# A decode block on one core: two bias vectors moved from the first load to sixteen short loads behind w1, and six other loads merged

## The chip, the cores and the metric

The program runs on one core of one Trainium2 chip. The metric is the device time of one execution in microseconds (us). It was run twice: 1054.84 and 1056.1 us, median 1055.47 us. A further execution was profiled; its own time was 1055.74 us and its span, from the first to the last instruction, 1053.9 us.

## The reference

One token passes through a transformer block with adaptive layer norms. Six modulation vectors come from a condition `c`. Attention has 32 heads of width 192 over a cache of 8192 positions; behind it comes a dense layer with a squared relu. All is float32.

```python
mod = (silu(c) @ w_mod).reshape(1, 6, 1, 640)
sa, ca, ga, sb, cb, gb = (mod[:, i] for i in range(6))
h = layernorm(x) * (1 + ca) + sa
q = (h @ wq) per head                    # 32 heads x 192
p = softmax(q . k_cache * 192 ** -0.5)   # over 8192 positions
x = x + ga * ((p @ v_cache) @ wo)
h = layernorm(x) * (1 + cb) + sb
f = max(h @ w1 + b1, 0) ** 2             # 640 -> 1536
x = x + gb * (f @ w2 + b2)               # 1536 -> 640
```

The key and value caches are by far the most of the data: 64 arrays of 6144 KB.

## The kernel before

**Staging.** Everything that is streamed goes through three large buffers (`slot`, line 53), 128 partitions of 14208 floats each. They are used in turn: the first load, then k0, v0, k1, v1 and so on to k31, v31, then `wm1_t`, `w1_t` and `w2_t`. A buffer can be loaded again only when the work on its old content is done. So wm1 follows v30 in its buffer, w1 follows k31, and w2 follows v31. All loads are issued from SyncE (SP) in program order and go into one DMA queue. A load of 128 partitions gives each partition one contiguous row.

**Counters of the loads.** The framework gives every load one of eight counters, DMAHW0 to DMAHW7, in turn: load number n (from 0) has counter n modulo 8. Who needs the data waits for that counter. Before SP issues a load on a counter, SP also waits until the load that had that counter last has landed, unless SP has already waited for it for another reason. A wait on SP holds back every load behind it in program order.

**A head (lines 201 to 275).** `keys` multiplies the head's keys by the query on VectorE (DVE, line 212) and sums the products on DVE, GpSimd (POOL) and ScalarE (ACT), in pieces that `SUMS` gives; the last head works in four pieces of 16 positions. `softmax` follows, `values` multiplies by the value cache on TensorE (PE, lines 248 and 252), and `own` brings the parts of the sums together. The key buffer of an odd head also holds a piece of `wo` behind the keys, which `gather` (line 154) uses; the last head's `gather` is what frees k31's buffer.

**How loads are cut.** `K_PARTS` cuts the key loads of the last two heads, line 98 the last value load in two, line 315 wm1 in two, `W1_CUT` w1 in two, and `W2_CUT` w2 in four pieces of 6, 3, 2 and 1 blocks. The sixth of the modulation matrix that makes `gb` (called wg here) has a load of its own behind w1, in w1's buffer (line 324).

**Biases.** `b1` and `b2` lie as 17 columns at the end of the first load. `bbc` (line 164) takes them out of its buffer, and `spread` (line 108: a copy and a transpose on DVE) makes them rows, `bbt`, at the start of the program (line 197).

**The end.** After the last head PE computes `ps_mod` from wm1 (line 335), the last attention sums and their projection `att` (341, 344), then, after a layer norm, `ps_f` from w1 (361). DVE adds `bbt`, squares and transposes to `fT` (364 to 366). PE computes `ps_g` from wg (371) and `ps_y` from w2 and `fT` (383); DVE makes `y`, and SP stores it (388). PE works in program order, so `ps_y` cannot start ahead of `ps_g`. Each matmul of float32 is two passes in the profile.

Of the kernel before, what the change touches and what calls it, by code (L numbers as in the profile page):

```python
# [14 lines left out]
D = 640  # L15
H = 32
SK = 8192
DH = 192
FF = 1536
# [3 lines left out]
KB = DG // 32  # L23
FB = FG // 32
PW = 2 * DH
NPAIR = H // 2
NPOS = SK // P
KV = NPOS * DH
WO = 3 * D
WQ = KB * PW  # L30
ROW = KV + WO
WM = KB * 2 * D
VEC = 3 * KB + FB
DA = 128
DB = DH - DA
REP = 8
K_PARTS = {H - 2: 2, H - 1: 4}
SUMS = {H - 3: ((14, 10), (14, 6)), H - 2: ((14, 12), (14, 8)), H - 1: ((4, 7), (4, 7), (4, 7), (4, 5))}
W1_CUT = ((0, 3), (3, 2))
W2_CUT = ((0, 6), (6, 3), (9, 2), (11, 1))  # L40
EPS = 1e-5


@with_exitstack
def block_kernel(ctx: ExitStack, tc: tile.TileContext, first, kx, vx, wm1, w1, w2, out):
    nc = tc.nc
    const = ctx.enter_context(tc.tile_pool(name="const", bufs=1))
    strm = ctx.enter_context(tc.tile_pool(name="strm", bufs=3))
# [4 lines left out]
    def slot(name):  # L53
        return strm.tile([P, ROW], F32, tag="slot", name=name, bufs=3)

    def big(name, n):
# [3 lines left out]
    k_t, v_t = {}, {}  # L60
    first_t = slot("first_t")
    nc.sync.dma_start(first_t[:, :WM + WQ + VEC], first)

# [11 lines left out]
                            axis=AX.X, op=ALU.add)  # L75
# [3 lines left out]
                            axis=AX.X, op=ALU.add)  # L79
# [3 lines left out]

    vec = first_t[:, WM + WQ:WM + WQ + VEC]
    c_c = vec[:, :KB]
    x_c = const.tile([P, KB], F32, name="x_c")
    bbc = const.tile([P, FB + KB], F32, name="bbc")

    def load_k(h):
        k_t[h] = slot(f"k{h}")  # L90
        n = K_PARTS.get(h, 1)
        cuts = [KV * c // n for c in range(n)] + [ROW if h not in (1, H - 2) else KV]
# [2 lines left out]

    def load_v(h):
        v_t[h] = slot(f"v{h}")
        cuts = (0, NPOS * DA, KV) if h == H - 1 else (0, KV)
        for a, b in zip(cuts, cuts[1:]):
            nc.sync.dma_start(v_t[h][:, a:b], vx[h, :, a:b])  # L100

    def columns(src, n, name, pool=const, **how):

# [4 lines left out]
    def spread(src, n, name):  # L108

        t = work.tile([P, FB + KB, 32], F32, name=name + "_c", tag="spread", bufs=1)  # L110
        nc.vector.tensor_copy(t[:, :n], src[:, :, None].to_broadcast([P, n, 32]))
        r = const.tile([P, 32 * n], F32, name=name)
        nc.vector.transpose(r, t[:, :n].rearrange("p b r -> p (b r)"))
        return r
# [46 lines left out]
    nc.vector.reciprocal(e, e)  # L161
    nc.vector.tensor_mul(e, e, c_c)
    nc.vector.tensor_copy(x_c, vec[:, KB:2 * KB])
    nc.vector.tensor_copy(bbc, vec[:, 2 * KB:])

    ma_w = big("ma_w", 2 * D)
    weigh(ma_w, first_t[:, :WM].rearrange("p (b n) -> p b n", b=KB))
# [26 lines left out]

    query(0, first_t[:, WM:WM + WQ])
    x_t = spread(x_c, KB, "x_t")
    bbt = spread(bbc, FB + KB, "bbt")

    ri_t, o_t, sp_t, os_t, sum_t = {}, {}, {}, {}, {}

# [22 lines left out]
    def softmax(h, sc):  # L223
        mp = work.tile([P, 1], F32, tag="mp", name=f"mp{h}")
        nc.vector.tensor_reduce(mp, sc, axis=AX.X, op=ALU.max)  # L225
        ps = psum.tile([P, 512], F32, tag="sm", name=f"ps_mx{h}", bufs=2)
        nc.tensor.transpose(ps[:, :P], mp.to_broadcast([P, P]), ident)  # L227
        nm = work.tile([P, 1], F32, tag="nm", name=f"nm{h}")
        nc.vector.tensor_reduce(nm, ps[:, :P], axis=AX.X, op=ALU.max, negate=True)  # L229

        p = work.tile([P, NPOS, REP], F32, tag="p", name=f"p{h}", bufs=1)
        i = h // 2
        if h % 2 == 0:
            sp_t[i] = work.tile([P, 2], F32, tag="sp", name=f"sp{i}")
        nc.scalar.activation(p, sc[:, :, None].to_broadcast([P, NPOS, REP]), AF.Exp, bias=nm,  # L235
                             accum_out=sp_t[i][:, h % 2:h % 2 + 1])
        if h % 2:
            sum_t[i] = total(sp_t.pop(i), f"sum{i}")
        return p
# [48 lines left out]
    for h in range(H):  # L288
        i = h // 2
        if h:  # L290
            load_k(h)
        load_v(h)

        def wo():
            if h % 2 and i:
                gather(acc, k_t[h][:, KV:ROW].rearrange("p (j n) -> p j n", j=3), oT_t.pop(i - 1))

        def between():
            if h % 2 == 0 and i + 1 < NPAIR:
                query(i + 1, k_t[h][:, KV:ROW])  # L300
            if h < H - 1:
                wo()

        sc = keys(h, between)
        p = softmax(h, sc)
        if h:
            own(h - 1)
        if h % 2 == 0 and h:
            oT_t[i - 1] = turn(i - 1)
        if h == H - 1:  # L310
            wo()
        values(h, p)

    M = 3 * D
    N1 = WO + (KB // 2 + 1) * M
    wm1_t = slot("wm1_t")
    for a, b in ((0, N1), (N1, WO + KB * M)):
        nc.sync.dma_start(wm1_t[:, a:b], wm1[:, a:b])
    wo_t = wm1_t[:, :WO].rearrange("p (j n) -> p j n", j=3)
    wm1_t = wm1_t[:, WO:WO + KB * M].rearrange("p (b m n) -> p b m n", b=KB, m=3)  # L320
    w1_t = slot("w1_t")
    for b0, n in W1_CUT:
        nc.sync.dma_start(w1_t[:, b0 * FF:(b0 + n) * FF], w1[:, b0 * FF:(b0 + n) * FF])
    nc.sync.dma_start(w1_t[:, KB * FF:KB * (FF + D)], w1[:, KB * FF:])
    wg_t = w1_t[:, KB * FF:KB * (FF + D)].rearrange("p (b n) -> p b n", b=KB)
    w1_t = w1_t[:, :KB * FF].rearrange("p (b n) -> p b n", b=KB)
    w2_t = slot("w2_t")
    for b0, n in W2_CUT:
        nc.sync.dma_start(w2_t[:, b0 * D:(b0 + n) * D], w2[:, b0 * D:(b0 + n) * D])
    w2_t = w2_t[:, :FB * D].rearrange("p (b n) -> p b n", b=FB)  # L330

    ps_mod = psum.tile([P, 512], F32, tag="q", name="ps_mod", bufs=2)
    for b in range(KB):
# [25 lines left out]
    for b in range(KB):  # L359
        for g in range(G):  # L360
            nc.tensor.matmul(pf[32 * g:32 * (g + 1), :FG], hT2[:, b], w1_t[:, b, FG * g:FG * (g + 1)],
                             start=(b == 0), stop=(b == KB - 1))
    f = work.tile([P, FG], F32, name="f", tag="spread", bufs=1)
    nc.vector.tensor_add(f, pf[:, :FG], bbt[:, :FG])
    nc.vector.scalar_tensor_tensor(f, f, 0.0, f, op0=ALU.max, op1=ALU.mult)
# [66 lines left out]
```

## Time and profile before

| | |
|---|---|
| two runs | 1054.84 and 1056.1 us, median 1055.47 |
| profiled execution, its own time | 1055.74 us |
| its span | 1053.9 us, so 1.84 us of its time lie outside |
| DVE busy | 898.9 us, 85% of the span |
| PE busy | 364.5 us, 35% |
| POOL busy | 187.7 us, 18% |
| ACT busy | 107.0 us, 10% |
| data moved | 452.17 MB, 429 GB/s over the span |
| mean granted PE clock | 0.653 |

The page of the profile gives the busy time of each engine, the span in 40 slices with the DMA's share and rate in each, the chain of work that ended last, and for every kind of load how many there were, how large each is and how long it took from issue to landing. The timeline gives instructions in order of time; in brackets stands how long an engine sat idle before one, and what ended that. Rows of the same kind are merged, with their count behind an x. KB are 1024 bytes and MB a million bytes. The windows give busy time, granted PE clock (1.00 is full, 0.50 half) and DMA rate for a stretch of time.

### The profile page before, as it was taken

The numbers are of one execution on the slowest core, as the hardware profiler recorded it, in microseconds if no ns is written. First come the engines' busy times: TensorE is split into PE (matmuls) and PEld (weight loads), VectorE is DVE, ScalarE is ACT, GpSimd is POOL, SyncE is SP. The second block draws the span as 40 slices with busy tenths as digits, with TensorE's granted clock in tenths as the row PEclk, the third lists the DMA queues.
The fourth block names the chain that finished last, engine by engine and source line by source line (L and its number), as shares of the span: only waits on it lengthen the run. The fifth ranks groups of instructions, "written<-read, shape, count | busy, mean of one in ns | idle before, by whom it ended". The sixth has DMA issues, their size and how long they took to land.

```text
span 1053.9 us, 5606 instructions
## 1 busy us (share of the span) xinstructions
PE 364.5 (35%) x2120; PEld 133.2 (13%) x2120; DVE 898.9 (85%) x398; ACT 107.0 (10%) x462; POOL 187.7 (18%) x44
## 2 busy tenths in 40 slices
PE   0325323243431334333143432224343133433246
PEld 0101101011110111111011110101111011110113
DVE  6896899898989989898998988989888998889882
ACT  1010101010010101001000010101001010011320
POOL 0120222220222220122221022221022222021210
PEclk9766656666665666656666665666666566665668
DMA  9999999999999999999999999999999999999997
GB/s 404 436 417 442 423 428 437 433 438 433 429 435 435 435 437 429 432 433 437 430 438 431 433 432 437 434 437 431 435 427 437 433 436 433 429 435 426 423 421 334
DMA packets 11411, 452.17 MB, mean 429 GB/s; under 512 B 1269, under 2 KB 1273, under 8 KB 1657
## 3 DMA queue, kind: packets, MB, share of 16 engines
q1 hardware_dynamic: 11384, 451.83, 99.4%
q8 instruction: 16, 0.26, 0.1%
q14 instruction: 11, 0.08, 0.0%
HBM read 451.82 MB, written 0.00 MB: 429 GB/s over the span
## 4 chain that ended last, share of the span: by engine, by line
DMA 43%; DVE 41%; PE 13%; ACT 1%; issue 1%; POOL 1%; SPq 0%; DVEq 0%; ACTq 0%; POOLq 0%
DMA k<-in_kx 39%; DVE k L212 21%; DVE sc L217 9%; PE ps_o L248 8%; DVE sc L220 5%; DVE acc L154 4%; PE ps_o L252 3%; DMA w_t<-in_w 2%; DMA first_t<-in_first 1%; ACT p L235 1%; POOL k L213 1%; PE ps_sum L120 1%; PE ps_mx L227 1%; DVE ma_w L149 1%; PE ps_q L191 1%
## 5 line engine op out<-in xcount | busy, mean ns | idle before, releaser
L212 DVE TENSOR_TENSOR k<-k,qb 128x12288 f32<-128x12288 f32 (+2 forms) x37 | 415.4, 11227 | 95.1 <-DMA k<-in_kx 90.4
L213 POOL TENSOR_TENSOR k<-k 128x2688 f32<-128x2688 f32 (+2 forms) x37 | 186.4, 5038 | 826.6 <-DVE k L212 782.2
L227 PE MATMUL ps_mx<-ident,mp 128*128 128x128 f32 x32 | 15.2, 474 | 586.0 <-DVE mp L225 586.0
L217 DVE TENSOR_REDUCE sc<-k 128x32 f32<-128x6144 f32 (+6 forms) x37 | 202.9, 5483 | 1.3
L248 PE MATMUL ps_o<-v,p 128*32 128x512 f32 x1024 | 181.7, 874 | 2.6 <-ACT p L235 2.6
L216 ACT ACTIVATE jk<-k 128x192 f32<-128x192 f32 x178 | 62.1, 350 | 527.9 <-DVE k L212 513.2
L220 DVE TENSOR_REDUCE sc<-k 128x28 f32<-128x2688 f32 (+2 forms) x37 | 93.8, 2535 | 3.7 <-POOL k L213 3.7
L227 PEld LDWEIGHTS ps_mx<-ident,mp 128*128 128x128 f32 x32 | 5.8, 182 | 610.9 <-DVE mp L225 590.1
L274 DVE TENSOR_REDUCE os<-own 128x128 f32<-128x512 f32 x64 | 63.8, 1037 | 1.1
L252 PE MATMUL ps_o<-v,p 128*32 128x512 f32 x512 | 60.5, 592 | 0.0
L191 PE MATMUL ps_q<-k,hR 128*128 128x384 f32 x150 | 54.0, 509 | 2.0 <-DMA k<-in_kx 2.0
L248 PEld LDWEIGHTS ps_o<-v,p 128*32 128x32 f32 x1024 | 39.5, 152 | 115.2 <-issue 111.9
L235 ACT ACTIVATE p<-sc,nm 128x512 f32<-128x512 f32 x32 | 23.1, 721 | 294.8 <-DVE nm L229 168.1
L154 DVE SCALAR_TENSOR_TENSOR acc<-k,oT,acc 128x640 f32<-128x640 f32 x45 | 41.1, 914 | 1.1
L281 PE MATMUL ps_oT<-ones,os 128*128 128x1 f32 x96 | 27.2, 356 | 42.5 <-DVE os L274 30.3
L216 ACT ACTIVATION_READ_ACCUMULATOR jk<-k 128x1 f32 x178 | 33.2, 186 | 0.0
L191 PEld LDWEIGHTS ps_q<-k,hR 128*128 128x128 f32 x150 | 28.1, 194 | 30.7 <-issue 12.1
L281 PEld LDWEIGHTS ps_oT<-ones,os 128*128 128x128 f32 x96 | 23.3, 304 | 50.3 <-DVE os L274 33.6
L229 DVE TENSOR_REDUCE nm<-ps_mx 128x1 f32<-128x128 f32 x32 | 9.3, 291 | 18.2 <-PE ps_mx L227 18.2
L271 DVE SCALAR_TENSOR_TENSOR own<-ps_o,ri,mask 128x1024 f32<-128x1024 f32 (+1 forms) x17 | 20.7, 1216 | 3.0 <-PE ps_o L252 3.0
L252 PEld LDWEIGHTS ps_o<-v,p 128*32 128x32 f32 x512 | 15.3, 110 | 40.8 <-issue 40.8
L271 DVE SCALAR_TENSOR_TENSOR own<-ps_o,mask 128x1024 f32<-128x1024 f32 x16 | 19.4, 1214 | 0.0
(87 smaller groups left out, 122.8 us busy)
## 6 DMA issues: line engine op xcount, KB each, us to landing
k<-in_kx SPq DMA_DIRECT2D x29, 7104.0 KB, 27.2
v<-in_vx SPq DMA_DIRECT2D x31, 6144.0 KB, 23.1
k<-in_kx SPq DMA_DIRECT2D x1, 6144.0 KB, 24.9
k<-in_kx SPq DMA_DIRECT2D x2, 3072.0 KB, 21.9
k<-in_kx SPq DMA_DIRECT2D x3, 1536.0 KB, 14.5
first_t<-in_first SPq DMA_DIRECT2D x1, 4173.5 KB, 12.6
v<-in_vx SPq DMA_DIRECT2D x1, 4096.0 KB, 18.0
wm_t<-in_wm SPq DMA_DIRECT2D x1, 3840.0 KB, 19.6
```

Source lines behind the costliest of these rows:

```text
L154: nc.vector.scalar_tensor_tensor(to, w[:, j], s[:, j:j + 1], to, op0=ALU.mult, op1=ALU.add)
L191: nc.tensor.matmul(ps[:, :PW], hR[:, b], w[:, b], start=(b == 0), stop=(b == KB - 1))
L212: nc.vector.tensor_mul(pr, pr, q[:, None, :].to_broadcast([P, n, DH]))
L213: nc.gpsimd.tensor_add(pr[:, a:b, :DH // 2], pr[:, a:b, :DH // 2], pr[:, a:b, DH // 2:])
L216: nc.scalar.activation(jk, pr[:, i], AF.Copy, accum_out=s[:, i:i + 1])
L217: nc.vector.tensor_reduce(s[:, :a], pr[:, :a], axis=AX.X, op=ALU.add)
L220: nc.vector.tensor_reduce(s[:, a:b], pr[:, a:b, :DH // 2], axis=AX.X, op=ALU.add)
L248: nc.tensor.matmul(o_t[h][32 * g:32 * (g + 1), :512], p[:, 4 * c:4 * c + 4].rearrange("p e r -> p (e r)"), t[:, 512 * c:512 * (c + 1)], st ...
L252: nc.tensor.matmul(o_t[h][32 * g:32 * (g + 1), 512:], p[:, 8 * c:8 * c + 8, ::2].rearrange("p e r -> p (e r)"), t[:, 512 * (na + c):512 * ...
L271: nc.vector.scalar_tensor_tensor(m[:, lo:hi], o[:, lo:hi], scale, mask[:, lo:hi], op0=ALU.mult, op1=ALU.mult)
L274: nc.vector.tensor_reduce(r, m[:, x0:x1].rearrange("p (j d) -> p d j", d=r.shape[1]), axis=AX.X, op=ALU.add)
L281: nc.tensor.matmul(pt[:, j:j + 1], os_[:, P * j:P * (j + 1)], ones[:, :1], start=True, stop=True)
```

## The change

- `b1` and `b2` leave the first load, which has 17 columns fewer. They become an input `bb` of 128 rows of 17 floats (68 bytes a row), loaded straight into `bbc` by sixteen loads behind w1: one of 8 rows, and then of 1, 2, 3 up to 15 rows. The copy to `bbc` at the start is gone.
- `spread` of the biases moves from the start of the program to behind the matmuls of `ps_f`.
- wg leaves w1's buffer and its own load. It now lies ahead of w2 in one input `gw2`, and the first of the four loads there takes wg and w2's first 6 blocks together.
- k31 comes in two loads instead of four, v31 in one instead of two, wm1 in one instead of two, and w1 in one instead of two.

Leaving the biases aside, the end of the program has six loads fewer; with them ten more.

```diff
-VEC = 3 * KB + FB
+VEC = 2 * KB
-K_PARTS = {H - 2: 2, H - 1: 4}
+K_PARTS = {H - 2: 2, H - 1: 2}
-W1_CUT = ((0, 3), (3, 2))
...
-        cuts = (0, NPOS * DA, KV) if h == H - 1 else (0, KV)
-        for a, b in zip(cuts, cuts[1:]):
-            nc.sync.dma_start(v_t[h][:, a:b], vx[h, :, a:b])
+        nc.sync.dma_start(v_t[h][:, :KV], vx[h])
...
-    nc.vector.tensor_copy(bbc, vec[:, 2 * KB:])
...
-    bbt = spread(bbc, FB + KB, "bbt")
...
-    N1 = WO + (KB // 2 + 1) * M
     wm1_t = slot("wm1_t")
-    for a, b in ((0, N1), (N1, WO + KB * M)):
-        nc.sync.dma_start(wm1_t[:, a:b], wm1[:, a:b])
+    nc.sync.dma_start(wm1_t[:, :WO + KB * M], wm1)
...
     w1_t = slot("w1_t")
-    for b0, n in W1_CUT:
-        nc.sync.dma_start(w1_t[:, b0 * FF:(b0 + n) * FF], w1[:, b0 * FF:(b0 + n) * FF])
-    nc.sync.dma_start(w1_t[:, KB * FF:KB * (FF + D)], w1[:, KB * FF:])
-    wg_t = w1_t[:, KB * FF:KB * (FF + D)].rearrange("p (b n) -> p b n", b=KB)
+    nc.sync.dma_start(w1_t[:, :KB * FF], w1)
     w1_t = w1_t[:, :KB * FF].rearrange("p (b n) -> p b n", b=KB)
-    w2_t = slot("w2_t")
+    r0 = 0
+    for n in [8] + list(range(1, 16)):
+        nc.sync.dma_start(bbc[r0:r0 + n], bb[r0:r0 + n])
+        r0 += n
+    gw_t = slot("gw_t")
+    a = 0
     for b0, n in W2_CUT:
-        nc.sync.dma_start(w2_t[:, b0 * D:(b0 + n) * D], w2[:, b0 * D:(b0 + n) * D])
-    w2_t = w2_t[:, :FB * D].rearrange("p (b n) -> p b n", b=FB)
+        b = (KB + b0 + n) * D
+        nc.sync.dma_start(gw_t[:, a:b], gw2[:, a:b])
+        a = b
+    wg_t = gw_t[:, :KB * D].rearrange("p (b n) -> p b n", b=KB)
+    w2_t = gw_t[:, KB * D:(KB + FB) * D].rearrange("p (b n) -> p b n", b=FB)
...
+    bbt = spread(bbc, FB + KB, "bbt")
     f = work.tile([P, FG], F32, name="f", tag="spread", bufs=1)
```

**Order on SP.** The rows show what SP issues, at the end of the program, and the counters it waits for there. Before, from v31's second piece to the store of `y`; the numbers in tile names are the program's, and `_49` is only a part of the counters' names:

```order
L100 DMA v_2248<-in_vx 128x4096
L318 DMA wm_t<-in_wm 128x7680 [waits DMAHW7_49,PE_49]
L318 DMA wm_t<-in_wm 128x3840
L323 DMA w_t<-in_w 128x4608 [waits DMAHW1_49,DMAHW0_49,DMAHW2_49,DVE_49,DMAHW3_49,Activation_49,Pool_49]
L323 DMA w_t<-in_w 128x3072
L324 DMA w_t<-in_w 128x3200
L329 DMA w_t<-in_w 128x3840 [waits DMAHW5_49,DMAHW4_49,PE_49]
L329 DMA w_t<-in_w 128x1920
L329 DMA w_t<-in_w 128x1280
L329 DMA w_t<-in_w 128x640 [waits DMAHW6_49]
L388 DMA out_y<-y 4x160 [waits DMAHW7_49,DVE_49]
```

In the changed kernel w1's load (load 68, counter DMAHW4) comes first, then the sixteen bias loads (loads 69 to 84), then the four of `gw2` (85 to 88). The rows from the bias load of 5 rows (load 74) on:

```order
L319 DMA bbc<-in_bb 5x17 [waits DMAHW2_49]
L319 DMA bbc<-in_bb 6x17 [waits DMAHW3_49]
L319 DMA bbc<-in_bb 7x17 [waits DMAHW4_49]
L319 DMA bbc<-in_bb 8x17 [waits DMAHW5_49]
L319 DMA bbc<-in_bb 9x17 [waits DMAHW6_49]
L319 DMA bbc<-in_bb 10x17 [waits DMAHW7_49]
L319 DMA bbc<-in_bb 11x17 [waits DMAHW0_49]
L319 DMA bbc<-in_bb 12x17 [waits DMAHW1_49]
L319 DMA bbc<-in_bb 13x17 [waits DMAHW2_49]
L319 DMA bbc<-in_bb 14x17 [waits DMAHW3_49]
L319 DMA bbc<-in_bb 15x17 [waits DMAHW4_49]
L325 DMA gw_t<-in_gw 128x7040 [waits DMAHW5_49,PE_49]
```

The five bias loads ahead of these wait for nothing. The load of 5 rows has the counter of v31 (load 66), that of 6 rows the counter of wm1 (67), that of 7 rows the counter of w1 (68). From the load of 8 rows on, each has the counter of the bias load eight places ahead of it, and so has `gw2`'s first load.

**Order on PE.** The end of PE's program before, from the first matmul on w1:

```order
L361 MATMUL ps_f<-w_t,hT_2453 32x384 [waits DMAHW0_49,DVE_49,Activation_49]
L361 MATMUL ps_f<-w_t,hT_2453 32x384 x11
L361 MATMUL ps_f<-w_t,hT_2453 32x384 [waits DMAHW1_49]
L361 MATMUL ps_f<-w_t,hT_2453 32x384 x7
L371 MATMUL ps_g<-w_t,silu 32x160 [waits DMAHW2_49]
L371 MATMUL ps_g<-w_t,silu 32x160 x19
L383 MATMUL ps_y<-w_t,fT 32x160 [waits DMAHW3_49,DVE_49,Activation_49]
L383 MATMUL ps_y<-w_t,fT 32x160 x23
L383 MATMUL ps_y<-w_t,fT 32x160 [waits DMAHW4_49]
L383 MATMUL ps_y<-w_t,fT 32x160 x11
```

And in the changed kernel:

```order
L359 MATMUL ps_f<-w_t,hT_2458 32x384 [waits DMAHW4_49,DVE_49,Activation_49]
L359 MATMUL ps_f<-w_t,hT_2458 32x384 x19
L370 MATMUL ps_g<-gw_t,silu 32x160 [waits DMAHW5_49]
L370 MATMUL ps_g<-gw_t,silu 32x160 x19
L382 MATMUL ps_y<-gw_t,fT 32x160 [waits DVE_49,Activation_49]
L382 MATMUL ps_y<-gw_t,fT 32x160 x23
L382 MATMUL ps_y<-gw_t,fT 32x160 [waits DMAHW6_49]
L382 MATMUL ps_y<-gw_t,fT 32x160 x11
```

`ps_f` now waits for the whole of w1 (DMAHW4), and the wait for `gw2`'s first load (DMAHW5) stands ahead of `ps_g` instead of ahead of `ps_y`.

**Order on DVE.** The same place on DVE in the changed kernel, from the transpose that gives `ps_f` its operand:

```order
L102 STREAM_TRANSPOSE hT_2458<-ln_h 128x160 [waits DVE_49]
L108 COPY bbt_c<-bbc 128x544 [waits DMAHW4_49,DMAHW5_49,DMAHW3_49,DMAHW6_49,DMAHW2_49,DMAHW7_49,DMAHW1_49,DMAHW0_49]
L110 STREAM_TRANSPOSE bbt<-bbt_c 128x544 [waits DVE_49]
L363 TENSOR_TENSOR f<-ps_f,bbt 128x384 [waits DVE_49,PE_49]
L364 SCALAR_TENSOR_TENSOR f<-f 128x384 [waits DVE_49]
```

The copy and the transpose of the biases stood at the start of the program before, and now stand ahead of the addition that uses them; the copy waits for all sixteen bias loads.

More of the change, by code (lines that the diff above doesn't have):

```diff
@@ L44, in block_kernel @@
 @with_exitstack
-def block_kernel(ctx: ExitStack, tc: tile.TileContext, first, kx, vx, wm1, w1, w2, out):
+def block_kernel(ctx: ExitStack, tc: tile.TileContext, first, kx, vx, wm1, w1, bb, gw2, out):
     nc = tc.nc
@@ L416 @@
     arrays = {
-        "first": np.concatenate([rows(wm[:, :2 * D], KB), wq[0], column(c, KB), column(A_x, KB),
-                                 column(B_b1, FB), column(B_b2, KB)], axis=1),
+        "first": np.concatenate([rows(wm[:, :2 * D], KB), wq[0], column(c, KB), column(A_x, KB)], axis=1),
         "kx": kx,
@@ L421 @@
         "wm1": np.concatenate([wo[-1], rows(wm[:, 2 * D:5 * D], KB)], axis=1),
-        "w1": np.concatenate([rows(B_w1, KB), rows(wm[:, 5 * D:], KB)], axis=1),
-        "w2": rows(B_w2, FB),
+        "w1": rows(B_w1, KB),
+        "bb": np.concatenate([column(B_b1, FB), column(B_b2, KB)], axis=1),
+        "gw2": np.concatenate([rows(wm[:, 5 * D:], KB), rows(B_w2, FB)], axis=1),
     }
```

## The prediction

> **What bounds the kernel now.** I read the page first: the slices of the span, then the queue.
>
> ```profile
> span 1053.9 us, 5606 instructions
> GB/s 404 436 417 442 423 428 437 433 438 433 429 435 435 435 437 429 432 433 437 430 438 431 433 432 437 434 437 431 435 427 437 433 436 433 429 435 426 423 421 334
> q1 hardware_dynamic: 11384, 451.83, 99.4%
> ```
>
> The one queue of loads is busy for 99.4% of the span at 429 GB/s. As long as SP always issues the next load before the last one is through, the kernel is as long as its bytes. The end is what the change touches, so I read the chain of waits there.
>
> ```profile
> 1027.09 22.27 DMA w_t<-in_w
> 1049.41 0.75 PE ps_y L383 x16
> 1050.16 0.52 PE ps_y L383 x8
> 1050.71 0.33 DVE y L386
> ```
>
> The stream runs to 1050.1; the last piece of w2 is worth 0.52 us on PE, whose last pass ends at 1050.68, and 3.2 us follow (y, its store). So what counts is when the last bytes come, and whether PE can still use them at once. For the first I read what SP issues and when.
>
> ```profile
> 974.60 1.77 SPq L94 DMA_DIRECT2D k<-in_kx  x4
> 990.74 0.80 SPq L100 DMA_DIRECT2D v<-in_vx  x2
> 1003.07 0.80 SPq L318 DMA_DIRECT2D wm_t<-in_wm  x2
> 1022.96 0.80 SPq L323 DMA_DIRECT2D w_t<-in_w  x2
> 1023.81 0.42 SPq L324 DMA_DIRECT2D w_t<-in_w  x1
> 1026.24 1.78 SPq L329 DMA_DIRECT2D w_t<-in_w  x4
> 1051.42 0.65 SPq L388 DMA_DIRECT2D out_y<-y  x1
> ```
>
> And from issue to landing (the last column, in us):
>
> ```profile
> k<-in_kx SPq DMA_DIRECT2D x3, 1536.0 KB, 14.5
> k<-in_kx SPq DMA_DIRECT2D x1, 2496.0 KB, 23.1
> v<-in_vx SPq DMA_DIRECT2D x1, 2048.0 KB, 22.5
> wm_t<-in_wm SPq DMA_DIRECT2D x1, 3840.0 KB, 19.6
> w_t<-in_w SPq DMA_DIRECT2D x1, 1536.0 KB, 13.6
> w_t<-in_w SPq DMA_DIRECT2D x1, 1920.0 KB, 19.0
> first_t<-in_first SPq DMA_DIRECT2D x1, 4173.5 KB, 12.6
> ```
>
> Before, w2 is issued at 1026.24, while w1 is still coming: w1's second piece, issued at 1022.96 + 0.33 + 0.04 = 1023.33, lands at 1023.33 + 13.6 = 1036.9. SP is more than 10 us ahead of the stream.
>
> **The change part by part.**
>
> *The wait on SP.* This carries the forecast. SP's rows in the changed kernel show that the bias load of 7 rows waits for DMAHW4, which is w1's counter. So SP stands still until w1 has landed whole, at 1036.9. Behind it in SP's order stand eight more bias loads and all of `gw2`. When the wait ends, nothing but the seven short loads already issued is left in the queue: the stream runs dry. Before gw2 can be issued, SP issues nine bias loads (7 to 15 rows).
>
> What one costs is not in the trace. The nearest rows: 0.33 us for the first of a burst of 128-row loads, 0.42 to 0.48 us for each behind it (1.78 us for four), and 0.65 us for the one transfer of few rows, the store of 4 rows. I take 0.55, between the burst and the store: 9 × 0.55 = 4.95 us, bounds 9 × 0.33 = 3.0 and 9 × 0.65 = 5.9. Their own counter waits (8 rows on the first load of 8, 15 rows on that of 7, gw2 on the second of 8) ask for loads issued at least eight issues, some 4 us, earlier or queued right behind w1; the store's whole way, from 1051.42 to the end of the span at 1053.9, is at most 2.5 us, so they are met; I add up to 1 us to the upper bound in case the first ones land late behind w1. gw2's first load is issued at 1036.9 + 4.95 = 1041.9. Before, the same bytes were in the queue 15 us sooner.
>
> *The way of gw2's first load.* It starts into an empty queue, as the first load of the program does: 4173.5 KB (4.274 MB) in 12.6 us, of which 4.274 MB at 429 GB/s are 9.96 and 2.6 fixed. It has 7040 columns × 512 bytes = 3.604 MB: 8.4 + 2.6 = 11.0 us, landing at 1052.9 (before, w2's first piece landed at 1026.24 + 19.0 = 1045.2). The whole of gw2, 5.57 MB, is there at 1041.9 + 2.6 + 13.0 = 1057.5. Uncertainty of the fixed part 0.7 us either way.
>
> *PE behind it.* For this I read PE's timeline and its clock.
>
> ```profile
> 1018.50 5.95 PE L248 MATMUL ps_o<-v,p 128*32 128x512 f32 x32
> 1025.99 4.20 PE L335 MATMUL ps_mod<-wm_t,silu 128*32 128x480 f32 x40
> 1037.26 4.90 PE L361 MATMUL ps_f<-w_t,hT 128*32 128x384 f32 x40 [1.75 <-issue]
> 1041.97 1.54 PE L371 MATMUL ps_g<-w_t,silu 128*32 128x160 f32 x40
> 1045.41 1.84 PE L383 MATMUL ps_y<-w_t,fT 128*32 128x160 f32 x48 [1.90 <-DMA w_t<-in_w]
> ```
>
> ```profile
> 1022.00:1023.00 1.00, 1.00 (x12) 0.30 (x8) 0.96 (x3) 0.00 (x0) 0.00 (x0) 0.50 0.97 415
> 1023.00:1024.00 1.00, 1.00 (x12) 0.24 (x8) 0.26 (x1) 0.00 (x0) 0.00 (x0) 0.90 1.00 430
> 1033.00:1034.00 1.00, 0.54 (x2) 0.45 (x2) 0.37 (x3) 0.98 (x2) 0.00 (x0) 0.72 1.05 442
> 1039.00:1040.00 1.00, 1.00 (x12) 0.43 (x8) 0.00 (x0) 0.00 (x0) 0.00 (x0) 0.50 1.06 451
> 1040.00:1041.00 1.00, 1.00 (x15) 0.28 (x11) 0.00 (x0) 0.00 (x0) 0.00 (x0) 0.86 1.00 430
> ```
>
> The third column from the right is the granted clock. PE's work after gw2's first load is `ps_g` and the twelve blocks of `ps_y`: 40 + 96 = 136 passes. `ps_g` was run at full clock, 40 passes in 1.54 us with 0.3 for the last one's latency, 0.032 us a pass. But by then PE has idled: `ps_f` would end near 1044 and gw2 comes at 1052.9. Two bursts in the rows show what follows an idle stretch: the one that starts at 1018.50 is at half clock until about 1023.1, 4.6 us, and `ps_f`, from 1037.26, until 1040.3, 3.0 us; at 1033 the clock falls after 1 to 2 us with little work. So gw2's first passes run at half clock, 0.064 us each, for 3.0 to 4.6 us; with 3.8 that is 59 passes, and 77 × 0.032 = 2.5 for the rest: with 0.4 for release and latency 6.7 us (6.3 to 7.1). PE ends at 1052.9 + 6.7 = 1059.6. That is behind the last landing (1057.5 plus 0.5), so PE and not the stream sets the end: the three later pieces are there when PE comes to them. At full clock it would be 4.8 us, and the last piece would decide, with 1058.0.
>
> The Trainium skill (TensorE: Matmul & The Clock Gate, Part 1: The HAM clock gate (the "warmup" mystery)) has the clock at half by default, at full after a busy window of about 3.4 us, and back at half after an idle one; the 3.0 and 4.6 us of the trace lie around that figure. By 3.4 us this term would be 6.5 us, an estimate from that page, against 6.7.
>
> *The tail* is unchanged, 3.2 us.
>
> *wm1 and w1 in one load each.* wm1's first piece landed at 1003.07 + 19.6 = 1022.7, the second, 1.97 MB, 4.6 us later at 1027.3 by the rate. `ps_mod` started at 1026.0 and now starts near 1027.4: everything to `ps_f` comes some 1.5 us later, `ps_f` at 1038.8 instead of 1037.3, ending near 1043.7; w1 has landed by then. This costs nothing, since gw2 comes at 1052.9, nine us behind. If gw2 came on time (1045.2), the 1.5 us would still nearly fit.
>
> *k31 and v31 in fewer loads.*
>
> ```profile
> 995.40 3.35 DVE L212 TENSOR_TENSOR k<-k,qb 128x3072 f32<-128x3072 f32 x1
> 1005.52 3.35 DVE L212 TENSOR_TENSOR k<-k,qb 128x3072 f32<-128x3072 f32 x1
> ```
>
> DVE comes to k31's first quarter at 995.40 and to the third at 1005.52. The second quarter had landed by 976.4 + 14.5 = 990.9 and the last by 976.4 + 23.1 = 999.5 (976.4 is the end of the burst of issues), so two halves cost no wait. v31's last piece landed by 991.5 + 22.5 = 1014.0, and `values` starts at 1018.50: no wait either. Fewer loads may make the stream denser: slices 37 to 39 of the page, in which most of the extra pieces come, run at 426, 423 and 421 GB/s, against some 433 for the slices ahead, 2.3% of 79 us = 1.8 us. Five of the loads that go lie ahead of w1's end, of some eight extra ones there; the gain is between 0 and 1.2 us. I take 0.5, since slices of one load per buffer vary as much (417 to 442).
>
> *The biases' spread.*
>
> ```profile
> 28.45 0.72 DVE L111 COPY bbt_c<-bbc 128x544 f32<-128x544 f32 x1
> 29.20 0.74 DVE L113 STREAM_TRANSPOSE bbt<-bbt_c 128x544 f32<-128x544 f32 x1
> 34.61 12.96 DVE L212 TENSOR_TENSOR k<-k,qb 128x12288 f32<-128x12288 f32 x1 [4.67 <-ACT qb L193]
> 1042.22 0.56 DVE L364 TENSOR_TENSOR f<-ps_f,bbt 128x384 f32<-128x384 f32 x1 [5.07 <-PE ps_f L361]
> 1043.41 0.58 DVE L105 STREAM_TRANSPOSE fT<-f 128x384 f32<-128x384 f32 x1
> ```
>
> At the start its 1.46 us lay in time in which DVE waits for `qb` anyway, so taking it away brings nothing. At the end it waits for the last bias load, issued at about 1041.4 and there by 1043.9: `bbt` is ready at 1045.4 and `fT` 1.8 us later (1043.41 + 0.58 - 1042.22), at 1047.2, under the wait for gw2 (1052.9). Without that cover it would cost up to 2 us. The bias rows themselves (128 of 68 bytes) move while the queue is dry.
>
> *Sum.* 1036.9 + 4.95 + 11.0 + 6.7 + 3.2 = 1062.8; less 0.5: a span of 1062.3. With the 1.84 us by which the profiled execution's own time (1055.74) is over its span (1053.9): **1064.1 us**, 8.4 over that execution; the median of the two runs, 1055.47, lies 0.3 under it, less than the two differ.
>
> **The rivals.**
>
> *A: SP is not held up in time, and nothing is lost.* The counter wait is passed early, or SP gets through the sixteen loads before w1 is in: 1023.4 + 16 × 0.55 = 1032.2, under 1036.9. Then the stream has no gap and ends at 1050.1 as before; `ps_g` and `ps_y` start warm at 1045.3, reach the last piece at 1050.1 (4.8 us), and all that is left is the gain of 0.5: 1055.2 us, not slower. For it speaks that there is room for sixteen issues in that stretch; against it, that the wait stands in SP's rows, and that PE's `ps_f` shows the same counter as w1's.
>
> *B: the short loads go one after the other.* If each of the nine can only be issued when the one ahead is through, or the queue takes a full trip for each, at up to 2.5 us (the store's), the stretch is 9 × 2.5 = 22.5 us instead of 4.95: 1064.1 + 17.5 = 1081.6 us. It decides a verdict at 2% from 1.94 us a load on (9 × 1.39 = 12.5 more than the forecast). Against it speaks that in the rows neighbours have different counters. The Trainium skill (DMA: Bandwidth & Descriptors, Rules for kernel authors) says to merge many small transfers, since under 64 KB one pays mostly overhead, and its fixed part of about 2.0 us (Anatomy of one DMA) would make this case some 4.5 us shorter, an estimate from that page; no row here shows short loads behind one another.
>
> *C: PE keeps its clock or the fixed part is smaller.* Then the last landing decides: 1057.5 + 0.5 + 3.2 - 0.5 + 1.84 = 1062.5 us, inside my range.
>
> **How the numbers follow.** Forecast with C, its neighbour, 0.83, A 0.12, B 0.05. The bounds of the unknown costs below 1064.1: issue 2.0, fixed part 0.7, clock 0.4, loads 0.7, together 3.8 if all go one way; above it: 0.9 and 1.0, 0.7, 0.4, 0.5, together 3.5. With the 0.6 us that a run lies off its median the range is 1059.5 to 1068.5; A and B lie outside it with 0.17 together. A measurement tells about 2% (21 us) from no change; by that, A, the forecast and C are all within it: same 0.94, slower 0.05 (B), faster 0.01.
>
> **What would show it.** In SP's timeline the issues at line 319 break off after the load of 6 rows and go on when w1 has landed, near 1037; gw2's issue stands near 1042. The DMA rate falls to almost nothing from 1037 to 1043 or so. PE waits for gw2 some 9 us, `ps_g` runs at clock 0.50, and its last pass ends some 6.7 us after that landing. If the bias issues go through without a break, or gw2's issue comes before 1035, the forecast is wrong and A is right; if more than 1 us lies between bias issues, B is.

## The result and the profile after

The changed kernel took 1063.57 us (median of two runs, 1062.81 and 1064.33) beside 1055.47 before: a ratio of 1.0072, 95% interval 1.0056 to 1.0089. That is 8.1 us slower, clear of the noise, and within 2%. The profiled execution took 1064.33 us, its span 1062.5; the forecast had 1064.1 for the time and 1062.3 for the span.

The page of the changed kernel, the rows of the span, of the rate in 40 slices and of the queue:

```profile
span 1062.5 us, 5617 instructions
GB/s 400 445 413 426 443 426 439 429 441 436 420 442 427 437 431 438 435 430 432 430 441 430 436 432 429 437 435 434 434 429 437 432 435 433 437 420 414 441 408 211
q1 hardware_dynamic: 10776, 451.83, 98.6%
```

The bytes are the same, and so is the rate over most of the span. The last slice differs, 211 GB/s where it was 334: the loss is at the end. What SP issued there, in order of time:

```profile
1023.43 0.33 SPq L315 DMA_DIRECT2D w_t<-in_w  x1
1023.81 16.87 SPq L319 DMA_DIRECT2D bbc<-in_bb  x16
1040.78 1.83 SPq L325 DMA_DIRECT2D gw_t<-in_gw  x4
1059.78 0.62 SPq L387 DMA_DIRECT2D out_y<-y  x1
```

The sixteen bias loads stretch over 16.87 us, and gw2, which could have been issued at about 1026 (w2 was at 1026.24 before), is issued at 1040.78. What SP waited for at line 319 stands in the list of its waits (us in total, how often, the longest):

```profile
SPq L319 <- DMA w_t<-in_w: 8.8, 1, 8.8
SPq L319 <- DMA wm_t<-in_wm: 2.6, 1, 2.6
```

The longer one is the wait for w1's counter. The chain that ended last takes up there; the bias loads of 7, 8 and 15 rows, gw2, and PE behind it:

```profile
1023.43 13.93 DMA w_t<-in_w
...
1037.38 0.27 SPq L319
...
1037.69 0.30 SPq L319
...
1040.30 0.38 SPq L319
...
1040.78 10.77 DMA gw_t<-in_gw
1051.55 0.04 issue
1051.59 2.90 PE ps_g L370 x40
1054.48 4.56 PE ps_y L382 x96
1059.04 0.02 issue
1059.07 0.34 DVE y L385
```

So w1 lands at 1037.36; nine short issues take until 1040.68; gw2's first load takes 10.77 us; PE then works through its 136 passes without a further wait. The windows show the empty queue and the clock (the last three columns are granted clock, DMA share and GB/s):

```profile
1036.00:1037.00 1.00, 0.29 (x11) 0.00 (x0) 0.32 (x1) 0.29 (x1) 0.00 (x0) 1.00 0.01 0
1039.00:1040.00 1.00, 0.21 (x2) 0.12 (x2) 0.42 (x2) 0.26 (x1) 0.00 (x0) 0.91 0.02 2
1052.00:1053.00 1.00, 1.00 (x24) 0.72 (x20) 0.00 (x0) 0.00 (x0) 0.00 (x0) 0.50 1.03 435
1056.00:1057.00 1.00, 1.00 (x24) 0.73 (x20) 0.00 (x0) 0.00 (x0) 0.00 (x0) 0.55 0.00 0
```

From 1036 to 1041 the rate is 0 to 3 GB/s: only the end of w1 and the short loads move. From 1051.59 PE runs at half clock until 1056.9 (0.55 in that slice). The last piece of gw2 has landed by 1056.2, and PE works on until 1059.04: PE sets the end.

### The profile page after: what moved, and what is told of

Same layout as the page of the kernel before. It is cut to its first block, busy times and chain, and to the rows that moved or that the text cites. A ratio compares the mean times of both kernels' runs of the same rounds, so it can differ in the third digit from the quotient of the medians.

```text
span 1062.5 us, 5617 instructions
## 1 busy us (share of the span) xinstructions
PE 374.7 (35%) x2120; PEld 136.1 (13%) x2120; DVE 898.9 (85%) x397; ACT 107.0 (10%) x462; POOL 187.7 (18%) x44
## 4 chain that ended last, share of the span: by engine, by line
DMA 42%; DVE 41%; PE 13%; ACT 1%; issue 1%; POOL 1%; SPq 0%; DVEq 0%; ACTq 0%; POOLq 0%
DMA k<-in_kx 39%; DVE k L207 21%; DVE sc L212 9%; PE ps_o L243 8%; DVE sc L215 5%; DVE acc L151 4%; PE ps_o L247 2%; DMA w_t<-in_w 1%; DMA first_t<-in_first 1%; ACT p L230 1%; DMA gw_t<-in_gw 1%; POOL k L208 1%; PE ps_mx L222 1%; PE ps_sum L117 1%; DVE ma_w L146 1%
## 5 line engine op out<-in xcount | busy, mean ns | idle before, releaser
L243 PE MATMUL ps_o<-v,p 128*32 128x512 f32 x1024 | 187.3, 898 | 2.6 <-ACT p L230 2.6
L247 PE MATMUL ps_o<-v,p 128*32 128x512 f32 x512 | 60.5, 592 | 0.0
L187 PEld LDWEIGHTS ps_q<-k,hR 128*128 128x128 f32 x150 | 28.1, 194 | 30.8 <-issue 12.4
```

Source lines behind the costliest of these rows:

```text
L187: nc.tensor.matmul(ps[:, :PW], hR[:, b], w[:, b], start=(b == 0), stop=(b == KB - 1))
L243: nc.tensor.matmul(o_t[h][32 * g:32 * (g + 1), :512], p[:, 4 * c:4 * c + 4].rearrange("p e r -> p (e r)"), t[:, 512 * c:512 * (c + 1)], st ...
L247: nc.tensor.matmul(o_t[h][32 * g:32 * (g + 1), 512:], p[:, 8 * c:8 * c + 8, ::2].rearrange("p e r -> p (e r)"), t[:, 512 * (na + c):512 * ...
```

## The experiments

Theory W is the forecast: SP stands at w1's counter, the queue runs dry, and gw2 and PE come late. Theory S is the rival that the sixteen short loads cost by themselves. Each kernel is the changed one with the edit shown, unless it says otherwise; each was timed beside the kernel before on the same chip, where that had medians of 1056.09 to 1056.43 us. Ratios are to the kernel before.

| run | median us | ratio, 95% interval |
|---|---|---|
| one bias load | 1055.91 | 1.0002 (0.9993 to 1.0011) |
| six bias loads | 1056.17 | 1.0001 (0.9993 to 1.0010) |
| seven bias loads | 1059.93 | 1.0033 (1.0021 to 1.0046) |
| biases in the first load | 1056.45 | 1.0001 (0.9993 to 1.0010) |
| sixteen from POOL | 1062.22 | 1.0055 (1.0042 to 1.0068) |
| twenty-four bias loads | 1066.02 | 1.0092 (1.0078 to 1.0106) |
| kernel before with the sixteen | 1064.33 | 1.0076 (1.0062 to 1.0089) |
| PE kept busy, 120 passes | 1064.36 | 1.0071 (1.0058 to 1.0085) |
| PE kept busy, 192 passes | 1064.74 | 1.0075 (1.0063 to 1.0088) |
| wg apart, wm1 in two | 1056.06 | 0.9999 (0.9990 to 1.0008) |
| sixteen of 8 rows | 1063.49 | 1.0067 (1.0055 to 1.0080) |
| the change again | 1062.97 | 1.0067 (1.0053 to 1.0080) |

**One, six and seven bias loads.** The counters decide which load of gw2 meets w1's.

```diff
-    for n in [8] + list(range(1, 16)):
+    for n in [P]:                       # one
+    for n in [16] * 4 + [32] * 2:       # six
+    for n in [16] * 6 + [32]:           # seven
```

> The changed kernel with the biases in one load of 128 rows instead of sixteen. Theory W (the wait of SP for w1's counter empties the queue): with one load nothing on SP waits for w1, gw2 is issued near 1025, the stream has no gap. What is left is the chain behind wm1, which in the changed kernel came 3.7 us later than before (ps_f started at 1040.96 instead of 1037.26): fT near 1049, ps_y near 1052.5, 1057.3 us in all (1055.2 if that chain is hidden). Theory S (the short loads cost by themselves, in the queue and in SP, in proportion to their number): 1/16 of the 8.1 us over the kernel before, 1056.0 us. Both are far below the changed kernel's 1063.6; the timeline of SP tells whether gw2 is issued before w1 lands.

> The changed kernel with the biases in six loads (four of 16 rows, two of 32). Theory W: gw2's first load now has wm1's counter and waits only until about 1028, its second has w1's and waits until 1037.4, while the first is still coming: no gap in the stream, the time of the one-load kernel within 0.5 us (1057.3). Theory S: 6/16 of 8.1, 1058.5 us, and half a us under the kernel with seven loads.

> The changed kernel with the biases in seven loads (six of 16 rows, one of 32): one load more than the kernel with six, but now gw2's first load has w1's counter. Theory W: SP holds gw2 back until w1 has landed at 1037.4, without the nine short issues behind it: gw2 lands first at 1037.4 + 10.8 = 1048.2, PE is warm from ps_f, 4.8 us for its 136 passes, 1053.0, and 1058.9 us in all: 1.5 us or more over the kernel with six loads, and 4.7 under the changed kernel (3.4 for the nine issues, the rest because PE does not run at half clock). Theory S: 7/16 of 8.1, 1059.0 us, half a us over the kernel with six loads. The step from six to seven, and SP's timeline, tell them apart.

With one load the time is that of the kernel before (1055.91 beside 1056.15); gw2 was issued at 1025.77, far ahead of w1's landing. Theory S had 1056.0, so this run alone does not tell the two apart. Theory W's 1057.3 was too high for one load and for six: the clock did not fall under `ps_mod` in either profile (4.23 us), so the chain behind wm1 came earlier than expected.

From six loads to seven the time steps by 3.8 us (1056.17 to 1059.93); theory S had half a us, and 3.0 us over the kernel before for six loads, where there is nothing. With seven, both theories had some 1059, which the profiled execution met (1058.97); the median is 1 us above. SP's timeline with six loads, bias loads and gw2:

```profile
1024.02 2.80 SPq L319 DMA_DIRECT2D bbc<-in_bb  x6
1028.59 10.51 SPq L325 DMA_DIRECT2D gw_t<-in_gw  x4
```

And with seven:

```profile
1022.79 4.62 SPq L319 DMA_DIRECT2D bbc<-in_bb  x7
1036.39 1.87 SPq L325 DMA_DIRECT2D gw_t<-in_gw  x4
```

With six, gw2's first load goes out at 1028.59, and SP stands at w1's counter only between it and the second (10.51 us for four issues), while 3.6 MB are under way. With seven, the same wait stands ahead of all of gw2. PE in the run with seven:

```profile
1047.21 2.59 PE L370 MATMUL ps_g<-gw_t,silu 128*32 128x160 f32 x40 [4.41 <-DMA gw_t<-in_gw]
1049.56 4.16 PE L382 MATMUL ps_y<-gw_t,fT 128*32 128x160 f32 x96
```

It waited 4.41 us and then took 6.5 us, not the 4.8 expected of a warm PE, since `ps_f` had ended at 1042.8 already; against that, gw2 came at 1047.2 and not at 1048.2. So the wait alone, without the nine issues, is 3.5 us (1.0033) of the change's 7.1 to 7.6. The rest is in the two profiles the nine issues (3.4 us) and PE, which took 0.9 us longer behind gw2 in the change.

**The fewer loads alone.** The biases go back to the first load, their copy and spread to the start, and `bb` is gone; all other loads stay merged.

```diff
-VEC = 2 * KB
+VEC = 3 * KB + FB
...
+    nc.vector.tensor_copy(bbc, vec[:, 2 * KB:])
...
-    for n in [8] + list(range(1, 16)):
-        nc.sync.dma_start(bbc[r0:r0 + n], bb[r0:r0 + n])
-        r0 += n
...
```

> The fewer loads alone: the biases are back in the first load, their spread is back at the start, and nothing is loaded between w1 and gw2; k31, v31, wm1, w1 and gw2 stay cut as in the changed kernel. By the prediction's terms it gains 0 to 1.2 us (1054.3 to 1055.5). By the trace of the changed kernel the chain behind wm1 starts with its whole landing (1028.3) and meets a clock that has fallen to half, so fT comes near 1049 and the time is near 1057.3. ps_mod's start and the clock under it tell.

Measured was no difference to the kernel before. Against the second expectation, the clock had not fallen under `ps_mod` here, so `fT` came at 1046.4, not 1049. The chain of waits shows how little was to spare; in order of time, from wm1 on:

```profile
1003.10 24.20 DMA wm_t<-in_wm
1027.34 4.23 PE ps_mod L331 x40
...
1038.28 6.31 PE ps_f L357 x40
...
1045.80 0.59 DVE fT L102
1046.52 3.50 PE ps_y L379 x96
```

In this profile the end hangs on wm1's landing and the row of small steps behind it, and no longer on the last load. (With one bias load the chain still runs through gw2.) The merged loads bring nothing that can be measured and have used up the cover of that chain.

**The sixteen loads from POOL's queue.**

```diff
-        nc.sync.dma_start(bbc[r0:r0 + n], bb[r0:r0 + n])
+        nc.gpsimd.dma_start(bbc[r0:r0 + n], bb[r0:r0 + n])
```

> The changed kernel with the same sixteen bias loads, of the same rows, issued from POOL instead of SP, where loads have counters of their own; POOL's last work on the keys ends near 1015, so it is free. Theory W: SP no longer waits for w1 and issues gw2 near 1026, so nothing is lost: 1056.2 us, as with the biases in one load. Theory S (sixteen short loads cost in the DMA queues whoever issues them): 1063.6 us, as the changed kernel.

Neither time came: 1062.22 is 6.0 us over W's and 1.4 under S's. On SP theory W held: gw2 was issued at 1027.39. But POOL has eight counters of its own, and the ninth load waits for the first. POOL's timeline:

```profile
1015.35 4.25 POOL L319 DMA_DIRECT2D bbc<-in_bb  x8
1023.01 0.52 POOL L319 DMA_DIRECT2D bbc<-in_bb  x1 [3.42 <-DMA bbc<-in_bb]
...
1038.42 0.52 POOL L319 DMA_DIRECT2D bbc<-in_bb  x1 [0.54 <-DMA bbc<-in_bb]
```

The list of issues has the size of each and the time from issue to landing, here beside SP's full stream; the first and the last of those listed:

```profile
bbc<-in_bb POOLq DMA_DIRECT2D x1, 0.5 KB, 17.2
...
bbc<-in_bb POOLq DMA_DIRECT2D x1, 1.0 KB, 9.4
```

The last is issued at 1038.42 and lands at 1047.8. DVE, and then PE:

```profile
1047.94 0.72 DVE L108 COPY bbt_c<-bbc 128x544 f32<-128x544 f32 x1 [9.09 <-DMA bbc<-in_bb]
```

```profile
1046.17 1.56 PE L370 MATMUL ps_g<-gw_t,silu 128*32 128x160 f32 x40 [2.28 <-DMA gw_t<-in_gw]
1051.45 5.14 PE L382 MATMUL ps_y<-gw_t,fT 128*32 128x160 f32 x96 [3.71 <-DVE fT L102]
```

gw2 is there at 1046.1, as in an undisturbed stream, and `ps_g` runs at once; `ps_y` waits for the biases. That the loss is nearly as large as the change's is chance; its cause is another, eight counters and late biases.

**Twenty-four and sixteen even loads.** What one more issue costs, and whether the uneven rows matter.

```diff
-    for n in [8] + list(range(1, 16)):
+    for n in [5] * 16 + [6] * 8:        # twenty-four
+    for n in [8] * 16:                  # even
```

> The changed kernel with the biases in 24 loads (sixteen of 5 rows, eight of 6). The counter of w1 falls on the eighth again, so seventeen instead of nine issues stand between w1's landing and gw2's issue. Theory W with the price from the changed kernel's trace (0.27 us for 7 rows to 0.38 for 15, and 0.04 between): 17 x 0.30 = 5.1 instead of 3.4 us, 1065.3 us. With the price of the prediction, 0.55 each, it would be 17 x 0.55 = 9.4 and 1069.5 us. Rival B of the prediction (each load waits for the one ahead, some 2 us) would give 1063.6 + 8 x 2 = 1079.6 us.

> The changed kernel with sixteen bias loads of 8 rows each instead of 8 and 1 to 15. The counter of w1 still falls on the eighth load and nine issues follow its landing. Theory W, with the issue times of the changed kernel's trace (0.27 us for 7 rows, 0.38 for 15): nine of 0.28 and 0.04 between instead of 3.4 us in all, 2.9: 0.5 us less than the changed kernel, 1063.1 us. If the uneven row counts themselves cost (they put 16 rows on some DMA engine and none on another), it is more than 1.5 us less.

Twenty-four cost 1.0092 against 1.0067 for the change timed again: 2.6 us for eight issues more, 0.33 each. Two rows of the chain, the last short issue (6 rows) and gw2:

```profile
1041.62 0.29 SPq L319
...
1042.01 10.71 DMA gw_t<-in_gw
```

0.29 and the 0.04 to 0.05 between make 0.33 to 0.34; one after the other at 2 us (rival B) is ruled out. SP's list of waits at line 319 names no short load either, here or in the change, only wm1 and w1. Sixteen even loads are equal to the change (both 1.0067), so the uneven rows do not cost the 1.5 us of the other expectation. The expected 0.5 us is too small for these runs to show; in the profile the nine issues took 3.1 us instead of 3.4.

**The sixteen loads in the kernel before.** All cuts of the kernel before, the biases out of the first load, the sixteen loads between wg and w2, the spread behind `ps_f`.

```diff
...
+    r0 = 0
+    for n in [8] + list(range(1, 16)):
+        nc.sync.dma_start(bbc[r0:r0 + n], bb[r0:r0 + n])
+        r0 += n
     w2_t = slot("w2_t")
...
+    bbt = spread(bbc, FB + KB, "bbt")
...
```

> The other part alone: k31, v31, wm1, w1, wg and w2 are cut and loaded as in the kernel before, and the sixteen bias loads stand behind w1 and wg, with their spread behind ps_f. Now the counters of w1's two pieces and of wg fall on the sixth to eighth bias load; SP waits until wg has landed, near 1041, and eight bias loads and w2 follow: w2's first issue near 1041 + 9 x 0.37 = 1044.3, its first piece lands 2.6 + 4.6 us later at 1051.5, and PE, idle since ps_g at 1043.5, needs 96 passes at half clock for up to 5.4 us, 5.8 in all: 1057.3 + 3.4 + 1.84 = 1062.5 us. Theory S: 1063.6 us or more, since the loads that the change takes away are still there. If it were the merged loads that cost, this kernel would be at 1056.

1064.33 us, as much as the whole change; so the fewer loads are not what costs. The chain of this run, the first short issue behind wg's landing, w2 and PE:

```profile
1040.55 0.27 SPq L327
...
1045.10 7.05 DMA w_t<-in_w
1052.15 0.14 issue
1052.29 6.41 PE ps_y L386 x96
```

It is the same chain one load later: SP is held by wg (landed at 1040.5), w2 goes out at 1045.10. The median was 1.8 us over the expectation, the profiled execution (1063.74) 1.2: in it the issues took 1.2 us more than thought (one of them 1.50 us, for a reason that the profile does not give) and PE 0.6, while wg landed 0.5 earlier.

**PE kept busy.** Matmuls of w1 into a tile that nothing reads, between `ps_f` and `ps_g`; 15 rounds of four in one run, 24 in the other.

```diff
+    ps_w = psum.tile([P, 512], F32, tag="sm", name="ps_w", bufs=2)
+    for b in range(15):
+        for g in range(G):
+            nc.tensor.matmul(ps_w[32 * g:32 * (g + 1), :DG], hT2[:, b % KB], w1_t[:, b % KB, DG * g:DG * (g + 1)],
+                             start=(b == 0), stop=(b == 14))
```

> The changed kernel with 60 further matmuls of w1 (120 passes, some 3.9 us) on PE between ps_f and ps_g, into a tile that nothing reads: they fill PE's idle time from 1047.2 to 1051.1, ahead of gw2's landing at 1051.55. If the half clock costs what the trace says (ps_g and ps_y took 7.4 us instead of some 4.9), the time falls by 2.5 us to 1061.1 us. If the last landing of gw2 had set the end anyway, as in rival C of the prediction, it falls by less than 1 us. If PE's clock is of no account, nothing changes (1063.6 us).

> The changed kernel with 96 further matmuls (192 passes, 6.2 us) instead of 60 between ps_f and ps_g, into a tile that nothing reads: in the run with 60 they ended 3.9 us ahead of gw2's landing, and the clock still fell, in the middle of ps_y. With 192 they end between 1050.6 and 1053.4 (ps_f ended at 1044.4 in one run and at 1047.2 in another); gw2 lands near 1051.6 to 1052.5. If an idle stretch ahead of the work is what halves the clock, ps_g and ps_y now run at full clock throughout, 4.9 us instead of 6.5 to 7.4, and the time is 1062 us (61.1 where the added work ends ahead of the landing, up to 1063 where it ends behind). If the clock falls for another reason, it is 1064 us or more.

> The changed kernel itself once more, with more executions, as the base for the runs with added matmuls and for sixteen loads of 8 rows: theory W and theory S both expect 1063.6 us; if it lies at 1064.5 or above, the two kernels with a warm PE saved up to 0.5 us, and if it lies near 1063 they saved nothing.

Neither was faster than the change (1.0071 and 1.0075 against 1.0067), so the expected 2.5 and 1.5 us did not come. With 120 passes the added work ended 3.9 us ahead of gw2 and the clock fell during the real work, as two windows show:

```profile
1052.00:1053.00 1.00, 0.46 (x16) 0.49 (x20) 0.00 (x0) 0.00 (x0) 0.00 (x0) 1.00 0.95 399
1054.00:1055.00 1.00, 1.00 (x21) 1.00 (x16) 0.10 (x1) 0.29 (x1) 0.00 (x0) 0.50 0.92 371
```

With 192 the clock stayed at 1.00 from 1047 to the end. PE in that run:

```profile
1046.63 6.71 PE L370 MATMUL ps_w<-w_t,hT 128*32 128x160 f32 x192
1053.15 1.56 PE L375 MATMUL ps_g<-gw_t,silu 128*32 128x160 f32 x40
1054.51 1.82 PE L387 MATMUL ps_y<-gw_t,fT 128*32 128x160 f32 x44
1057.30 2.10 PE L387 MATMUL ps_y<-gw_t,fT 128*32 128x160 f32 x52 [0.98 <-issue]
```

`ps_g` was quick again (1.56 us instead of 2.90). But the added matmuls changed more than the clock. From issue to landing gw2's first load took 10.7 to 10.8 us in the five other profiles in which it started into an empty queue (the change, the change again, seven, twenty-four and even loads). Here it took 12.0 us with 120 passes and 12.4 us with 192, where it landed at 1053.0. SP and PE with 120 passes:

```profile
1040.42 1.88 SPq L325 DMA_DIRECT2D gw_t<-in_gw  x4
1052.54 2.00 PE L375 MATMUL ps_g<-gw_t,silu 128*32 128x160 f32 x40 [3.87 <-DMA gw_t<-in_gw]
```

The trace records the landing of a load in sixteen parts. In both runs fifteen of them were in by 1051.4, and the last came 1.0 and 1.6 us behind. In both a packet of 16 KB of instructions was loaded while gw2 was on its way (some 0.9 us of one transfer, from 1047.4 with 120 passes and from 1049.1 with 192); in the five other profiles none was. That the longer program's own code held up one part of gw2 is therefore likely, and it is not shown.

With 192 passes PE also stopped for 0.98 us after 44 of the 96 passes of `ps_y`. The profile does not name what ended that stop. It was not gw2's second load, which had landed at 1055.3, a us before the stop began.

So these two runs do not show what the half clock is worth in the changed kernel: what they took from PE's time they added in front of it. With the stop taken off, the 136 passes took 5.1 us at full clock in the run with 192, against 7.5 in the change; by these two figures it would be some 2 us, an estimate. The change timed again lies at 1062.97, near the 1063 at which its expectation has the added matmuls saving nothing.

**A version meant to beat both.** One bias load, k31, v31 and w1 merged, wm1 in two pieces, wg in a load of its own ahead of w2.

```diff
-    nc.sync.dma_start(wm1_t[:, :WO + KB * M], wm1)
+    N1 = WO + (KB // 2 + 1) * M
+    for a, b in ((0, N1), (N1, WO + KB * M)):
+        nc.sync.dma_start(wm1_t[:, a:b], wm1[:, a:b])
...
-    for n in [8] + list(range(1, 16)):
+    for n in [P]:
...
-    a = 0
+    a = KB * D
+    nc.sync.dma_start(gw_t[:, :a], gw2[:, :a])
```

> A version meant to beat both: the biases in one load of 128 rows behind w1, the fewer loads of k31, v31 and w1 kept, wm1 in two pieces as before, and wg in a load of its own ahead of w2, so that ps_g is done before w2 comes and only 96 passes stand behind w2's first piece. In the kernels with nothing held back the last piece landed near 1049.3 to 1049.7, against 1050.1 before, and PE's 136 passes behind gw2's first load used that up. If that is where the gain of the fewer loads went, this kernel ends 0.4 to 0.8 us before the kernel before (1055.4 beside 1056.2); if the stream decides, it is equal.

0.9999: it beats neither the kernel before nor the one-load version. The stream decides: in the profile PE's last 24 passes waited for a load of gw2 that landed at 1049.7.

## Why the prediction was right

Its steps, one by one, in the profile of the change; the terms sum to 1037.36 + 3.42 + 10.77 + 7.49 + 3.46 = 1062.5.

- **The wait on SP** is shown: SP stopped after the load of 6 rows, for 8.8 us, and went on at 1037.4 (forecast 1036.9). The step from six to seven loads shows that the place of w1's counter is the cause, and the number of short loads by itself is not.
- **The nine issues** were over-sized: 3.4 us, not 4.95. Each takes 0.27 to 0.38 us, like the first of a burst of 128-row loads. The store's 0.65 was no measure for a short load.
- **gw2's first load** took 10.8 us (11.0).
- **PE behind it** was under-sized in this profile: 7.5 us from the landing to PE's end, over the upper bound of 7.1. Half clock lasted 5.3 us of it, where the bounds had 3.0 to 4.6. When the same kernel was profiled again, the term was 7.0 us and half clock lasted 4.3, both inside the bounds. So the size varies between executions of one kernel, and two bursts were too few to bound it. That PE and not the last landing sets the end was right for the change.
- **The tail** was 3.5 us (3.2): from PE's end at 1059.04 to the end of the span.
- **wm1 in one load** was hidden, as forecast, but moved more than said in this profile: `ps_f` started at 1040.96, 3.7 us later than before and not 1.5. `ps_mod` started 2.3 us later (wm1 had been issued 1.7 us later, at 1004.79), and the clock fell under it (5.93 us where it was 4.20). So PE waited 4.4 us for gw2 and not some 9. In the second profile `ps_mod` took 4.23 us, `ps_f` started at 1037.96, and PE waited 7.63. "Would still nearly fit" holds: with the biases in the first load that chain sets the end, without loss.
- **The biases' spread** was hidden, as forecast: `bbt` was ready at 1043.7, ahead of `ps_f`, and `fT` at 1049.0, ahead of gw2 at 1051.55.
- **The gain from fewer loads**, 0.5 us, did not show (1.0001).
- **Rival A** did not happen in the change: gw2 was issued at 1040.78. Where nothing holds gw2 back, its "not slower" is right (one and six loads, as before), but its gain of 0.5 us did not show. **Rival B** is out at 0.33 us a load; the way of the last short load, issued at 1040.30, was over by 1042.15, when the copy that waits for it starts, so even a whole trip was under 2 us. **Rival C** did not happen either: PE ran at half clock, and its end lies 2.8 us behind the last landing.

The three rows of PE in the second profile of the changed kernel:

```profile
1037.96 5.01 PE L359 MATMUL ps_f<-w_t,hT 128*32 128x384 f32 x40 [1.75 <-DVE hT L102]
1050.60 2.90 PE L370 MATMUL ps_g<-gw_t,silu 128*32 128x160 f32 x40 [7.63 <-DMA gw_t<-in_gw]
1053.27 4.21 PE L382 MATMUL ps_y<-gw_t,fT 128*32 128x160 f32 x96
```

The mechanism was right: the wait, the empty queue, the late gw2 and PE behind it. That the sum came within 0.3 us of the measured span is luck: the issues were 1.5 us too much and gw2's way 0.2, while w1's landing was 0.4 too little, PE 0.8, the tail 0.3, and the gain of 0.5 was not there.

## What to carry to other kernels

A short load costs little by itself (0.33 us on the issuing queue here), but each one takes a turn of a small ring of completion counters, and the turn that meets a long load still on its way stops everything behind it on that queue. Count the loads between a long load and the next one that must not be late: here six were free, seven cost 3.5 us and sixteen 7 to 8. Moving them to another queue only moves the question: that queue has its own ring, and short loads there took 9 to 17 us to land beside a full stream.

## What the runs showed of the hardware that was not expected

- The issue of a short load on SP grows a little with its rows: 0.29 to 0.30 us for 5 to 9 rows (0.27 where it is the first behind a wait) and 0.38 for 15, but 0.33 for the first of 128 rows.
- Loads of 0.5 to 1.0 KB from POOL's queue took 9.4 to 17.2 us to land beside SP's stream.
- In all fourteen profiles the granted clock changes only at instants whose distances are multiples of 3.41 us, in the change at 1039.83, 1046.65, 1050.07 and 1056.89. How long PE worked at half clock behind an idle stretch, before the clock rose again, differed with the moment at which it took up work: from 3.0 us (`ps_f` in the kernel before) to 6.0 us (`ps_y` in the kernel before with the sixteen loads, from 1052.29 to 1058.26).
- In the run with 120 added passes the clock fell only after PE had taken up work again, 1.0 us into it, behind an idle stretch of 3.9 us.
